# A gated residual in one VectorE pass, one-column statistics on GpSimd, and a new literal order list

## The chip, the cores and the metric

The kernel runs on one core of a Trainium2 chip. The metric is the time of one execution in microseconds on the device (us); lower is better. The engines have short names in the profile: PE is TensorE (matmuls), PEld its weight loads, DVE is VectorE, ACT is ScalarE, POOL is GpSimd, SP is SyncE, which issues nearly all DMA transfers.

## The reference

The input x has 2048 tokens of 640 channels, in fp32. Two layers follow one another, each made of a gated long convolution (A) and a two-matmul MLP (B), each with a layer norm ahead and a residual around it:

```python
def _layernorm(x, axis=-1, eps=1e-5):
    m = jnp.mean(x, axis=axis, keepdims=True)
    v = jnp.var(x, axis=axis, keepdims=True)
    return (x - m) / jnp.sqrt(v + eps)
def _A_ref(q, k, v, shift_k, ssm_k, ssm_D):
    # k_shift: causal depthwise convolution of k, 4 taps
    kv = k_shift * v
    # y: causal depthwise convolution of kv with ssm_k, 2048 taps, by FFT
    y = y + kv * ssm_D[None, None, :]
    return q * y
def _B_ref(x, w1, w2):
    h = jnp.maximum(jnp.einsum("bsd,df->bsf", x, w1), 0)
    return jnp.einsum("bsf,fd->bsd", h, w2)

x = A_q
x = x + _A_ref(_layernorm(x), A_k, A_v, A_shift_k, A_ssm_k, A_ssm_D)
x = x + _B_ref(_layernorm(x), B_w1, B_w2)
x = x + _A_ref(_layernorm(x), A_k, A_v, A_shift_k, A_ssm_k, A_ssm_D)
x = x + _B_ref(_layernorm(x), B_w1, B_w2)
```

The convolution's result y does not depend on x, so both layers use the same y. w1 is 640 x 1728 and w2 is 1728 x 640.

## The kernel before, in words

**Tiles and stages.** The tokens are cut into 8 chunks of 256, each chunk into two halves of 128 tokens (the 128 partitions); channels lie along the free dimension, 640 columns. The statistics of a layer norm are therefore single columns: one number for each token.

- `transform` (tiles kt, acc, tp, sd, pt, sh, pr, at; hf, hr, gs, pg, ob, gt) brings k, v and the long filter into transform space, unit by unit (a chunk and some of its five blocks of 128 channels). `products` multiplies and accumulates there on DVE (pd, pacc; the factors of earlier chunks come back from DRAM as Ax and Gx), and brings y back (u, pq, ys). For chunk 0 ("direct") y is used on the spot; otherwise it is written to DRAM (Y) and read back as the tile y when it is needed; the last blocks of a chunk can be taken straight from ys (`near`).
- `norms` and `wsplit` (ws, w, "ones" sums) scale the MLP weights and split them into fp16 pairs. The MLP runs as three fp16 matmuls per product (high x high, high x low, low x high).
- `prep` makes one gated residual and the input of the following MLP: `stats` of the norm of A, the gate, the residual, `stats` of the norm of B, the split of the normed x into two fp16 halves (xh), and its transposition by DMA (xT).
- `main` is one MLP: h = xT w1 in 14 blocks (1728 = 13 x 128 + 64), each evicted from PSUM by a ReLU on ACT (hh) and a subtraction on DVE (the low half, hl, or for some blocks a combined form, both at line L1494), then o and oc = hh w2, added into x on DVE (L1585). For chunks 6 and 7 a form with fewer block products is used (ha, hs, gs, ek; L1268).

There are 20 mains, n = 0 to 19: chunks 0 and 1 in halves (layer 0 half 0, layer 0 half 1, layer 1 half 0, layer 1 half 1, for each chunk), and then the pairs (2,3), (4,5), (6,7), where each pair does layer 0 for both chunks and then layer 1.

**`stats`.** For each norm ACT makes negm (minus the mean, from row sums), ssq (a pass of squares of 640 columns into the scratch tile jk, with its row sum) and std (square root); DVE takes the reciprocal; then ACT refines 1/sqrt by one Newton step in one- and two-column passes (var, rstd, var, rstd, nmr; L1079 to L1083), one for each half where the scale is a column. ACT ends with the pass xn = r x + nmr (L1093), the normed x. There are tiles of both norms, A and B (xnA, xnB).

**The gate.** DVE multiplies xnA by y (L1136; L906 for the direct chunk), and a second DVE pass adds the product to x and sums the rows into sums2 for the norm of B (L1143). The first norm of a chunk in layer 0 gets its row sums from a pass over x on ACT (jq, L1104); in layer 1 the sums come from the additions of the MLP, whose two parts one ACT step adds (sums, L1593).

**Order.** Every operation is registered with `plan` with its engine, its reads, its writes and a priority. `best`/`order` run a list scheduling over them, whose priorities come from a table (RANKS), and `issue` emits all operations in that order. Each engine has one in-order queue: an operation that waits holds up all behind it. POOL's queue holds set-up work and 40 accumulating DMA issues (L554, L668; 20 each), which wait for their inputs there, and two late additions (L1522). At the start PE runs 38 small matmuls on an identity ("spin", L1602), the first 8 matmuls of pg, and 10 and 8 more spins (L1619) around pt, ahead of pr.

Of the kernel before, what the change touches and what calls it, by code (L numbers as in the profile page):

```python
# [1747 lines left out]
```

## Time and profile before

| what | value |
| --- | --- |
| three runs | 843.01, 843.47, 843.5 us; median 843.47 |
| profiled execution, span on the core | 841.6 us |
| median over that span | 1.9 us |
| instructions in the profile | 20268 |
| granted PE clock | 1.00 in every stage |
| DMA | 181.69 MB, 216 GB/s on average |

The span of the profiled execution runs from the first to the last instruction that the profiler recorded; no time of its own for that execution is given beside it, so the span is set against the median of the runs. Four views are used below: the page with the engines' busy time and the chain of work that ended last; the table of waits (who waited for whom: total, times, longest); windows (busy time of PE, PEld, DVE, ACT, POOL, each with its number of instructions, then the granted clock, the DMA share and GB/s); and groups of instructions by line (busy time, mean ns of one, idle time ahead and what ended it). Times are microseconds from the start of the span.

### The profile page before, as it was taken

What the parts mean: (1) busy time and instruction counts of PE and PEld (TensorE: products, weight loads), DVE (VectorE), ACT (ScalarE), POOL (GpSimd) and SP (SyncE); (2) the same over time, 40 slices, a digit from 0 to 9 for tenths busy, and PEclk for the clock granted to TensorE, in tenths of its full rate; (3) what the DMA queues carried; (4) which work ended last, traced back from release to release, by engine and by line L of the source; (5) the groups of instructions that cost most, each with busy time, mean ns of one, the idle gap of its engine ahead of it and who ended that gap; (6) DMA issues with size and microseconds to landing.
All of it is one profiled execution on the core that took longest, in us unless ns stands there. A gap on an engine that the chain in (4) does not pass through costs nothing.

```text
span 841.6 us, 20268 instructions
## 1 busy us (share of the span) xinstructions
PE 833.6 (99%) x8031; PEld 669.3 (80%) x8031; DVE 786.8 (93%) x1431; ACT 522.8 (62%) x1237; POOL 45.5 (5%) x56
## 2 busy tenths in 40 slices
PE   8999999999999999999999999999999999999998
PEld 7987887888888778777787777777777788888887
DVE  6999999999999999999999999999988799998775
ACT  5798887347776586647438574655524487868432
POOL 0000000000002111011110201010000000000000
PEclk9999999999999999999999999999999999999999
DMA  8995877987999997988998967688987466250400
GB/s 300 395 355 170 259 211 226 309 307 257 266 249 266 327 252 212 239 248 221 235 267 238 244 218 182 159 209 256 255 271 268 110 202 141 79 104 2 58 33 33
DMA packets 138145, 181.69 MB, mean 216 GB/s; under 512 B 53825, under 2 KB 95681, under 8 KB 138050
## 3 DMA queue, kind: packets, MB, share of 16 engines
q1 hardware_dynamic: 129586, 169.81, 67.4%
q0 software_dynamic: 8320, 10.49, 7.9%
q8 instruction: 63, 1.03, 0.5%
q14 instruction: 32, 0.26, 0.1%
q10 hardware_dynamic: 144, 0.10, 0.0%
HBM read 124.59 MB, written 34.08 MB: 189 GB/s over the span
## 4 chain that ended last, share of the span: by engine, by line
PE 79%; DVE 12%; DMA 3%; ACT 3%; issue 2%; SPq 0%; DVEq 0%; ACTq 0%
PE o L1268 10%; PE h L1350 8%; PE h L1351 8%; PE h L1353 8%; PE o L1323 7%; PE o L1322 7%; PE o L1325 6%; PE h L1338 4%; PE h L1383 2%; PE hs L1383 2%; PE h L1340 2%; PE oc L1322 2%; PE oc L1323 2%; PE oc L1325 2%; DVE pd L803 2%
## 5 line engine op out<-in xcount | busy, mean ns | idle before, releaser
L1350 PE MATMUL h<-xT,w 128*128 128x256 f16 (+1 forms) x1000 | 229.4, 249 | 0.9 <-DVE hh L1494 0.9
L1353 PE MATMUL h<-xT,w 128*128 128x256 f16 (+1 forms) x1000 | 229.2, 249 | 0.0
L1351 PE MATMUL h<-xT,w 128*128 128x256 f16 (+1 forms) x1000 | 229.2, 249 | 0.0
L1322 PE MATMUL o<-w,hh 128*128 128x512 f16 x336 | 127.3, 379 | 0.0
L1323 PE MATMUL o<-w,hh 128*128 128x512 f16 x336 | 127.3, 379 | 0.0
L808 DVE TENSOR_TENSOR pacc<-pacc,pd 128x1536 f32<-128x1536 f32 (+1 forms) x75 | 123.2, 1642 | 0.5
L1351 PEld LDWEIGHTS <-w 128*128 128x128 f16 x1100 | 107.6, 98 | 16.0 <-issue 1.8
L1350 PEld LDWEIGHTS <-w 128*128 128x128 f16 x1100 | 107.6, 98 | 14.5
L1353 PEld LDWEIGHTS <-w 128*128 128x128 f16 x1000 | 97.8, 98 | 6.3
L1493 ACT ACTIVATE hh<-h 128x512 f16<-128x512 f32 (+1 forms) x97 | 46.9, 485 | 69.1 <-PE h L1353 29.3
L1322 PEld LDWEIGHTS <-hh 128*128 128x128 f16 x672 | 65.7, 98 | 26.5
L1323 PEld LDWEIGHTS <-hh 128*128 128x128 f16 x672 | 65.8, 98 | 25.9
L803 DVE TENSOR_TENSOR pd<-Ax,Gx 128x768 f32<-128x768 f32 x83 | 78.3, 950 | 4.4 <-DMA Gx<-G 4.1
L1325 PE MATMUL o<-w,hl 128*128 128x512 f16 x208 | 78.8, 379 | 0.0
L1322 PE MATMUL oc<-w,hh 128*128 128x128 f16 x336 | 73.8, 220 | 0.0
L1323 PE MATMUL oc<-w,hh 128*128 128x128 f16 x336 | 73.6, 219 | 0.0
L532 ACT ACTIVATE tp<-kt,shs 128x256 f32<-128x256 f32 (+1 forms) x78 | 44.0, 577 | 26.8 <-DVE acc L606 20.8
L1325 PEld LDWEIGHTS <-hl 128*128 128x128 f16 x416 | 40.7, 98 | 24.5
L1338 PE MATMUL h<-xT,w 128*128 128x256 f16 (+1 forms) x400 | 57.9, 251 | 0.0
L1325 PE MATMUL oc<-w,hl 128*128 128x128 f16 x208 | 45.6, 219 | 0.0
L803 DVE TENSOR_TENSOR pd<-at,Gx 128x768 f32<-128x768 f32 x46 | 43.0, 950 | 0.7 <-DMA Gx<-G 0.5
L1338 PEld LDWEIGHTS <-w 128*128 128x128 f16 x400 | 35.9, 98 | 5.1
(284 smaller groups left out, 2010.3 us busy)
## 6 DMA issues: line engine op xcount, KB each, us to landing
Ax<-A SPq DMA_DIRECT2D x89, 384.0 KB, 4.2
Gx<-G SPq DMA_DIRECT2D x89, 384.0 KB, 4.4
A<-at SPq DMA_DIRECT2D x14, 768.0 KB, 6.3
G<-gt SPq DMA_DIRECT2D x14, 768.0 KB, 5.3
ws<-in_w SPq DMA_DIRECT2D x28, 320.0 KB, 6.8
y<-Y SPq DMA_DIRECT2D x22, 320.0 KB, 3.8
x<-in_q SPq DMA_DIRECT2D x16, 320.0 KB, 4.9
gs<-in_hF SPq DMA_DIRECT2D x20, 256.0 KB, 4.4
```

The costliest lines, as they stand in the source:

```text
L532: ACT.activation(o[:, i : i + m], kview(i, m, j), AF.Copy, scale=shs[:, t, j : j + 1])
L803: ew(f"mac{j % POOLMOD}", 768, lambda e, x=dst[i], av=av, gv=gv: e.tensor_mul(x.t, av(), gv()), [ax, gx], [dst[i]], pr_)
L808: dve(768 * (hi - lo), lambda lo=lo, hi=hi, pd=pd: DVE.tensor_add(acc[:, lo:hi], acc[:, lo:hi], pd[:, lo:hi]), [*sums[lo:hi], *dst[lo:hi]] ...
L1268: PE.matmul(b[:, c : c + w], x, y[:, z : z + w], start=done[i] == 1, stop=end, skip_group_check=fin)
L1322: PE.matmul(z, hh[:, c], wh[:, d], start=(j == JS[0] and i == 0 and (h == 0 or s == S[0])), stop=False)
L1323: PE.matmul(z, hh[:, c], wl[:, d], start=False, stop=end and tail)
L1325: PE.matmul(z, hl[:, c], wh[:, d], start=False, stop=end)
L1338: PE.matmul(p[:, z], wh, xv(t, x), start=b and x == 0, stop=e and x == 1)
L1350: PE.matmul(p[:, z], wh, xv(t, 0), start=b, stop=False)
L1351: PE.matmul(p[:, z], wh, xv(t, 1), start=False, stop=tail and e)
L1353: PE.matmul(p[:, z], wl, xv(t, 0), start=False, stop=e)
L1493: act(2 * R, lambda pv_=pv_, hh=hh: ACT.activation(hh.t, pv_(), AF.Relu), [src], [hh], URGENT)
```

## The change

Four things change.

1. *The gated residual.* With m the mean and r the factor of the norm, x + (x - m) r y equals (x - m)(r y + 1) + m. ACT now makes t = r y + 1 out of y (scale r, bias one), in place of the pass xn; DVE makes x <- (x - m) t in one pass with its row sums; the multiplication by y goes. The m is left out of x, since the norm of B does not see it. It is kept in a small tile (`means`, one column for each half and chunk): layer 0 stores it, layer 1 adds its own mean to it, and 16 ACT passes of 640 columns (one for each half of each chunk, priority LATER) add it to x in layer 1, behind the norm of B.
2. *One-column statistics.* negm, the steps of the Newton refinement, nmr, the means and `sums` move from ACT to POOL, 252 operations in all, as `tensor_scalar` and `tensor_tensor` over one or two columns. ACT keeps squares and square root, DVE the reciprocal.
3. *Column sums of the weights.* The matrix of ones for the three matmuls of `norms` becomes bf16, with the upper half of each fp32 value as the other operand.
4. *The order.* The list scheduling and its table are taken out; the order of all operations is a literal permutation (ORDER).

On DVE 44 instructions fewer are issued; on ACT 305 one- and two-column passes and 32 passes xn fewer, and 44 passes t, 16 passes of the mean and one more table load (`ACT_TABLE_LOAD`; the first operation with another function now comes ahead of the first square root). PE's matmuls are the same, apart from point 3. SP issues the same 512 rows.

```diff
-RANKS = (
-    "D*!A2000311ONp91^@>D2mlEH3IGcL3;+!P4ge1T5C9PX5&#nb6aW<f762Cj7yuan8UPyr8~_~v9snNzAOIl%A^;-*BmgA<CIBY@C;$ThF90zBDF7`1E&wV3GypOHH2^jMIsiTZIRHHXK>$MlQUFu{"
...
+ORDER = (
+    "0{{d71po#B2LK2F2>=QJ3jhoN4FC=R4*(DV5dabZEC4S6DF7`1`~Uy|695zd6#xMMDgZD5E&wtBF#tROHUKvOX#fHMJpgS0ZU8?3"
...
+    def table(self):
+        return [self.ops[k] for k in np.frombuffer(base64.b85decode(ORDER), "<u2")]
     def issue(self):
-        out, end = self.best()
-        for o in out:
+        for o in self.table():
...
+    one = keep(const, [P, 1], "one")
+    POOL.memset(one.t, 1.0)
+    means = keep(const, [P, 2 * NC], "means")
...
         if direct:
-            xs, xns, sp0 = first[c]
+            xs, (r, negm), sp0 = first[c]
             for s in range(2):
-                dve(h, lambda s=s: DVE.tensor_mul(xns[s][:, cs], xns[s][:, cs], dst[s][:, cs]), ...)
-                dve(h, lambda s=s: DVE.scalar_tensor_tensor(xs[s][:, cs], xns[s][:, cs], 1.0, xs[s][:, cs], op0=ALU.mult, op1=ALU.add, accum_out=...), ...)
+                t = T(mlp, "xn", 2, [P, h], f"t{c}{s}{t0}")
+                act(h, lambda s=s, t=t: ACT.activation(t.t, dst[s][:, cs], AF.Identity, scale=r[:, s : s + 1], bias=one.t), ...)
+                dve(h, lambda s=s, t=t: DVE.scalar_tensor_tensor(xs[s][:, cs], xs[s][:, cs], negm[:, s : s + 1], t.t, op0=ALU.add, op1=ALU.mult, accum_out=...), ...)
...
-        ones = keep(const, [P, P], "ones")
+        ones = keep(const, [P, P], "ones", BF16)
...
-    def stats(xs, sums, name, S, pr=0, fine=False):
+    def stats(xs, sums, name, S, pr=0, gated=None):
...
-        act(2, lambda: ACT.activation(negm[:, q_], sums[:, q_], AF.Copy, scale=-1.0 / D), [sums], [negm], pr, 0.1)
+        plan.op("POOL", 0.12, lambda: POOL.tensor_scalar(negm[:, q_], sums[:, q_], -1.0 / D, None, op0=ALU.mult), [sums], [negm], pr)
...
-            (0.2, [ssq, heps], [v], lambda: A(v[:, q_], ssq[:, q_], ident_, scale=-0.5 / D, bias=heps.t)),
-            (0.19 * len(S), [v, sd], [r], lambda: [A(r[:, c], v[:, c], ident_, scale=sd[:, c]) for c in cols]),
...
+            ([ssq], v, lambda: TS(V(v), V(ssq), -0.5 / D, -0.5 * EPS, op0=ALU.mult, op1=ALU.add)),
+            ([v, sd], r, lambda: TT(V(r), V(v), V(sd), op=ALU.mult)),
+            ([r, sd], v, lambda: TT(V(v), V(r), V(sd), op=ALU.mult)),
+            ([v], v, lambda: TS(V(v), V(v), 1.5, None, op0=ALU.add)),
+            ([v, sd], r, lambda: TT(V(r), V(v), V(sd), op=ALU.mult)),
...
+        if gated is not None:
...
+                m = MEAN[a]
+                plan.op("POOL", 0.12, lambda: POOL.tensor_sub(m[:, q_], m[:, q_], negm[:, q_]), [negm, m], [m], FILL)
+            return r, negm
...
-                ew("ay", cut, lambda e, s=s, xn=xns[s]: e.tensor_mul(xn[:, 0:cut], ys[s][:, 0:cut], xn[:, 0:cut]), [ys[s], xns[s]], [xns[s]], URGENT)
+                gate_ = lambda o, i, s=s: ACT.activation(o, i, AF.Identity, scale=r[:, s : s + 1], bias=one.t)
+                act(cut, lambda s=s, t=t, gate_=gate_: gate_(t[:, 0:cut], ys[s][:, 0:cut]), [ys[s], r, one], [t], URGENT, 0.18)
...
-                dve(D, lambda s=s, xn=xns[s]: DVE.scalar_tensor_tensor(xs[s].t, xn.t, 1.0, xs[s].t, op0=ALU.mult, op1=ALU.add, accum_out=sums2[:, s : s + 1]), [xns[s], xs[s]], [xs[s], sums2], URGENT, 0.2)
+                dve(D, lambda s=s, t=t: DVE.scalar_tensor_tensor(xs[s].t, xs[s].t, negm[:, s : s + 1], t.t, op0=ALU.add, op1=ALU.mult, accum_out=sums2[:, s : s + 1]), [t, negm, xs[s]], [xs[s], sums2], URGENT, 0.2)
...
+        for s in S if layer else ():
+            act(D, lambda s=s: ACT.activation(xs[s].t, xs[s].t, AF.Identity, bias=MEAN[a][:, s : s + 1]), [xs[s], MEAN[a]], [xs[s]], LATER, 0.1)
...
-            act(2, lambda: [ACT.activation(sums[:, s : s + 1], sp[:, s, 0:1], AF.Identity, bias=sp[:, s, 1:2]) for s in S], [sp], [sums], URGENT, 0.1 + 0.2 * (len(S) - 1))
+            plan.op("POOL", 0.12, lambda: POOL.tensor_add(sums[:, q_], sp[:, q_, 0], sp[:, q_, 1]), [sp], [sums], URGENT)
```

Three places in the queues show what moves. In the names, `A0_1_0` stands for the norm of A of chunk 0, layer 1, half 0; the last number of a name is a serial number, and the line numbers of after are its own.

The first place is that norm on ACT, from its row sums to the pass of 640 columns that DVE needs. Before:

```order
L1593 ACTIVATE sums0_0_0_1467<-sp0_0_0_1448 128x1
L1068 ACTIVATE negmA0_1_0_1469<-sums0_0_0_1467 128x1
L1071 ACTIVATE jkA0_1_00_1476,ssqA0_1_0_1477<-x0_0_222,negmA0_1_0_1469 128x640
L1072 ACTIVATE stdA0_1_0_1487<-ssqA0_1_0_1477,epst_88 128x1
L663 ACTIVATE ob1_2_1489<-pg11_2_1474 128x512
L532 ACTIVATE tp11_4_1502<-kt1_4_1446,shs_94 128x256
L1498 ACTIVATE tl_86<-hb1_1491 64x128
L532 ACTIVATE acc1_4_1517<-kt1_4_1446,shs_94 128x256
L1079 ACTIVATE varA0_1_0_1535<-ssqA0_1_0_1477,heps_90 128x1
L1080 ACTIVATE rstdA0_1_0_1536<-varA0_1_0_1535,stdA0_1_0_1487 128x1
L1081 ACTIVATE varA0_1_0_1535<-rstdA0_1_0_1536,c15_91,stdA0_1_0_1487 128x1
L1082 ACTIVATE rstdA0_1_0_1536<-varA0_1_0_1535,stdA0_1_0_1487 128x1
```

Now, on ACT:

```order
L998 ACTIVATE jkA0_1_00_1451,ssqA0_1_0_1452<-x0_0_219,negmA0_1_0_1417 128x640
L999 ACTIVATE stdA0_1_0_1454<-ssqA0_1_0_1452,epst_88 128x1
L455 ACTIVATE tp11_4_1468<-kt1_4_1389,shs_93 128x256
L616 ACTIVATE sh1_2_1494<-pt1_2_1471 128x512
L373 ACTIVATE cGh_1500<-cG_167 128x512
L1075 ACTIVATE t0_1_00_1512<-y0_1_00_1114,one_90,rstdA0_1_0_1465 128x640
```

and on POOL, whose queue had held no work here:

```order
L1532 TENSOR_TENSOR sums0_0_0_1415<-sp0_0_0_1412 128x1
L995 TENSOR_SCALAR negmA0_1_0_1417<-sums0_0_0_1415 128x1
L1006 TENSOR_SCALAR varA0_1_0_1457<-ssqA0_1_0_1452 128x1
L1007 TENSOR_TENSOR rstdA0_1_0_1465<-varA0_1_0_1457,stdA0_1_0_1454 128x1
L1008 TENSOR_TENSOR varA0_1_0_1457<-rstdA0_1_0_1465,stdA0_1_0_1454 128x1
L1009 TENSOR_SCALAR varA0_1_0_1457<-varA0_1_0_1457 128x1
L1010 TENSOR_TENSOR rstdA0_1_0_1465<-varA0_1_0_1457,stdA0_1_0_1454 128x1
L995 TENSOR_SCALAR negmB0_1_0_1522<-sums20_1_0_1520 128x1
```

The steps from sums to rstd have moved to POOL, and between square root and t ACT's queue has three other passes where it had four and five small steps.

The second place is the gated residual of the same half on DVE, behind the reciprocal. Before:

```order
L1074 RECIPROCAL stdA0_1_0_1487<-stdA0_1_0_1487 128x1
L664 TENSOR_TENSOR gt1_2_1515<-pg01_2_1465,ob1_2_1489 128x2x2x128
L558 TENSOR_TENSOR gs01_4_1543<-hf1_4_1373,hr1_4_1368 128x256
L665 TENSOR_TENSOR gt1_2_1515<-pg01_2_1465,ob1_2_1489 128x2x2x128
L606 TENSOR_TENSOR acc1_4_1517<-acc1_4_1517,tp11_4_1502 128x256
L558 TENSOR_TENSOR gs11_4_1555<-hf1_4_1373,hr1_4_1368 128x256
L675 TENSOR_TENSOR gt1_2_1515<-gt1_2_1515 128x2x256
L1136 TENSOR_TENSOR xnA0_1_00_1553<-y0_1_00_1173,xnA0_1_00_1553 128x640
L606 TENSOR_TENSOR acc1_4_1517<-acc1_4_1517,tp21_4_1580 128x256
L1143 SCALAR_TENSOR_TENSOR x0_0_222,sums20_1_0_1600<-xnA0_1_00_1553,x0_0_222 128x640
```

Now:

```order
L1001 RECIPROCAL stdA0_1_0_1454<-stdA0_1_0_1454 128x1
L481 TENSOR_TENSOR gs01_4_1492<-hf1_4_1380,hr1_4_1442 128x256
L1433 SCALAR_TENSOR_TENSOR hh1_3_1445<-h1_3_1391,hh1_3_1445 128x256
L481 TENSOR_TENSOR gs11_4_1502<-hf1_4_1380,hr1_4_1442 128x256
L726 TENSOR_TENSOR pd1_0_2_1448<-at1_0_1214,Gx1_0_0_1_1153 128x768
L1080 SCALAR_TENSOR_TENSOR x0_0_219,sums20_1_0_1520<-x0_0_219,negmA0_1_0_1417,t0_1_00_1512 128x640
```

The two passes have become one, with four other passes between the reciprocal and it where there were seven.

The third place is the start of PE. Behind 38 spins it had:

```order
L636 MATMUL pg00_0_213<-hf0_0_163,cG_151 128x2x128 x4
L636 MATMUL pg10_0_228<-hf0_0_163,cG_151 128x2x128
L636 MATMUL pg10_0_228<-hf0_0_163,cX_200 128x2x128
...
L683 MATMUL pt0_0_260<-ident_76,sd0_0_243 128x128 x4
...
L698 MATMUL pr00_0_285<-sh0_0_279,cM_204 128x2x128 x2
```

and behind 19 spins it now has:

```order
L559 MATMUL pg00_0_185<-hf0_0_165,cG_167 128x2x128 x4
L559 MATMUL pg10_0_198<-hf0_0_165,cG_167 128x2x128
L559 MATMUL pg10_0_198<-hf0_0_165,cX_177 128x2x128
...
L606 MATMUL pt0_0_226<-ident_76,sd0_0_215 128x128 x4
...
L559 MATMUL pg10_2_249<-hf0_2_217,cG_167 128x2x128
...
L621 MATMUL pr00_0_310<-sh0_0_242,cM_221 128x2x128 x2
```

Half of the spins ahead of pg have moved behind it: five stand between pg and pt, four behind pt, and 28 between the next two matmuls of pg and pr. The list of loads on SP changes there too: the first piece of k and the filter now stand ahead of cG, x of the first half one place earlier, cM three places later.

More of the change, by code (lines that the diff above doesn't have):

```diff
@@ L364, in issue @@
             o.fn()
-        return end
 @with_exitstack
@@ L1633, in early @@
         sums = load_x(a)
-        first[a] = (X[a], stats(X[a], sums, f"A{a}_0", both, URGENT, True), [keep(const, [P, 1, 3], f"sp{a}_{s}") for s in range(2)])
+        first[a] = (X[a], stats(X[a], sums, f"A{a}_0", both, URGENT, (a, 0)), [keep(const, [P, 1, 3], f"sp{a}_{s}") for s in range(2)])
     early(0)
```

316 lines of the change are left out of this document (122 added, 194 removed).

## The prediction

> **What bounds the kernel now.** I read the page first, for the engines' shares and the chain that ended last; then what TensorE (PE) waits for; then busy time by stage; then the chain where it leaves PE. First the page's lines on engines and on the chain:
>
> ```profile
> PE 833.6 (99%) x8031; PEld 669.3 (80%) x8031; DVE 786.8 (93%) x1431; ACT 522.8 (62%) x1237; POOL 45.5 (5%) x56
> PE 79%; DVE 12%; DMA 3%; ACT 3%; issue 2%; SPq 0%; DVEq 0%; ACTq 0%
> ```
>
> PE is busy for 833.6 of 841.6 us, so at most 8.0 us of visible idle time is there to be won, whatever VectorE (DVE) is spared, as long as the matmuls stay. They do: the change alters no matmul but three small ones. Next, all that PE waits for:
>
> ```profile
> PE spin L1602 <- POOL heps L435: 1.9, 1, 1.9
> PE h L1350 <- DVE hh L1494: 0.9, 2, 0.6
> PE pg L636 <- DVE hf L538: 0.8, 2, 0.4
> PE oc L1325 <- DVE hh L1494: 0.3, 1, 0.3
> PE pr L698 <- ACT sh L693: 0.2, 1, 0.2
> ```
>
> The 1.9 is the start before anything can run, 0.8 + 0.2 belong to the start-up of the convolution, and 0.9 + 0.3 = 1.2 us are waits for DVE in the steady part. The stages (columns after the comma: PE, PEld, DVE, ACT, POOL) show where:
>
> ```profile
> 0.00:20.00 20.00, 17.04 (x116) 14.97 (x117) 13.08 (x31) 11.25 (x25) 1.81 (x14) 1.00 0.87 296
> 80.00:100.00 20.00, 19.70 (x183) 15.59 (x182) 19.46 (x41) 16.56 (x40) 0.00 (x0) 1.00 0.75 239
> 120.00:140.00 20.00, 19.12 (x236) 16.51 (x234) 18.78 (x39) 14.37 (x39) 0.00 (x0) 1.00 0.69 209
> 200.00:400.00 200.00, 199.94 (x1893) 157.26 (x1893) 198.14 (x313) 136.50 (x327) 19.94 (x20) 1.00 0.93 256
> 400.00:680.00 280.00, 280.00 (x2323) 213.47 (x2321) 264.12 (x378) 146.92 (x345) 22.03 (x21) 1.00 0.83 226
> 760.00:842.00 82.00, 77.75 (x950) 67.65 (x947) 59.54 (x167) 38.02 (x91) 1.69 (x2) 1.00 0.16 32
> ```
>
> DVE is nearly full from 80 to 400 us, but from 200 us on PE is full too. PE's holes lie in the first 20 us (2.96), in 80–140 (0.30 + 0.88 = 1.18) and in the last window (4.25, mostly the stores after the last matmul). The chain that ended last runs through ACT and DVE from 80 to about 235 us and through PE from there; its pieces at the first hole (start, length, what), and the removed multiplies that it holds later:
>
> ```profile
> 79.95 0.21 ACT negmA L1068
> 80.18 0.93 ACT jkA L1071 x2
> 83.14 0.19 ACT varA L1079
> 83.36 0.30 ACT rstdA L1080
> ...
> 84.43 0.30 ACT nmrA L1083
> 84.76 0.93 ACT xnA L1093
> 85.72 0.82 DVE xnA L1136
> 86.94 0.60 issue
> 108.68 0.74 DVE xnA L1136
> 132.81 1.28 DVE xnA L1136 x2
> 199.87 0.74 DVE xnA L1136
> ```
>
> The hole itself, at the end of that 1.28 (start, length, engine, what; in brackets the idle time before):
>
> ```profile
> 131.14 1.75 DVE L808 TENSOR_TENSOR pacc<-pacc,pd 128x1536 f32<-128x1536 f32 x1
> ...
> 134.01 0.41 DVE L1494 SCALAR_TENSOR_TENSOR hh<-h,hh 128x256 f16<-128x256 f32 x1
> 134.48 0.22 PE L1350 MATMUL h<-xT,w 128*128 128x128 f16 x1 [0.62 <-DVE hh L1494]
> 134.48 0.10 PEld L1351 LDWEIGHTS <-w 128*128 128x128 f16 x1 [0.90 <-issue]
> ```
>
> The split of h (L1494), for which PE waits, stands on DVE right behind two of the multiplies that go. The weight loads idle 0.90 where PE's column says 0.62: idle time counts only from the modelled end of the last matmul, so the real hole is up to 0.28 larger, and holes shorter than that do not show.
>
> **The change, part by part.** *DVE.* Prices of the pass that goes and of the one that stays:
>
> ```profile
> L1136 DVE TENSOR_TENSOR xnA<-y,xnA 128x640 f32<-128x640 f32 x22 | 17.7, 819 | 0.9 <-ACT xnA L1093 0.8
> L1143 DVE SCALAR_TENSOR_TENSOR x<-xnA,x 128x640 f32<-128x640 f32 x30 | 24.4, 815 | 0.0
> ```
>
> 22 full multiplies are 17.7 us; 22 narrower ones (128 to 512 columns) I count by columns: 4 of 384, 4 of 512, 8 of 256, 6 of 128 is 6,400 columns, or 10 times 640, so 10 x 0.82 = 8.2 us. Some 26 us of DVE work goes in all. The pass x <- x + xnA becomes (x - mean) x t, in the same form and size, at 815 ns: no change. Off the path 26 us are worth nothing; on it they are worth PE's holes. Both visible waits (1.2) are for DVE, and the chain holds 0.82 + 0.74 + 1.28 + 0.74 = 3.58 us of removed passes before 235 us. So the term has the ends 0 (another DVE instruction ends last there) and -3.6. With three recorded waits, each up to 0.28 short, the holes are 1.2 + 3 x 0.28 = 2.0, and small ones come on top; I take **-2.4**. Late next there is PE itself.
>
> *ACT.* 305 one- and two-column steps leave. In the chain above they take from 83.14 to 84.73, 1.6 us for one half of a chunk. The normalising pass (0.93) is replaced by t = r y + 1 of the same width: equal. Sixteen passes x + mean (640 columns, so about 0.93 each, 15 us) come late in layer 1 at a low priority. ACT is 62% busy and 136.50 of 200 in the fullest long stage; the steps that left cover them. Without that cover, one such pass ahead of the ReLU eviction would delay PE by 0.93 us. A second table load, at the start, lies in ACT's idle time before 20 us. I count 0.
>
> *GpSimd (POOL).* 252 small operations come, in one queue with 40 DMA issues. The trace has no such operation; its nearest rows:
>
> ```profile
> L1522 POOL TENSOR_TENSOR x<-x,ek 128x320 f32<-128x320 f32 x2 | 1.7, 862 | 213.6 <-ACT ek L1519 213.6
> L433 POOL MEMSET epst<- 128x1 f32 x1 | 0.1, 98 | 0.0
> L554 POOL DMA_DIRECT2D gs<-hr x20 | 20.0, 1001 | 328.4 <-DVE x L1585 214.4 <-ACT hr L553 44.1 <-DVE gt L664 34.2
> 835.57 1.13 DVE L1431 SCALAR_TENSOR_TENSOR x<-o,winv,x 128x320 f32<-128x320 f32 x2
> ```
>
> One column costs between 0.10 (a write of one column) and 0.86 (two inputs, 320 columns). A linear reading of the two, 0.10 + 2/320 of the rest, stays near 0.1; a two-input step has some start-up, so I take 0.15. Five steps are then 0.75 us against ACT's 1.6, about 0.8 us less on each stretch from squares to t. At 0.86 they would be 4.3, or 2.7 us more. Behind an accumulating DMA of L554 a step waits 1.0 us for its issue at most, if that DMA's inputs have landed; the stages show no POOL work between 80 and 140 us, where PE's holes are, and 20 instructions in 200 to 400, where it has none. A DMA standing ahead with late inputs would hold the steps longer. Both I count 0.
>
> The Trainium skill speaks against this part: "SBUF — State Buffer", section "Who interferes with whom", says that a DVE instruction with two SBUF inputs contends with a GpSimd instruction that reads SBUF, whoever issues first keeping the shared port to its end. By this rule DVE, which is nearly full with such passes, would hold up most small steps by half a pass or so, which is rival B below. In this trace the two L1431 passes that run at 835.57, over the start of the two-input L1522, take 1.13 together, their usual 0.54 each; but one of their inputs is an output of PE, so no run here shows the case.
>
> *Order and start.* The literal order puts 19 of the 38 warm-up matmuls ahead of the first convolution matmuls, the others behind. Rows of the start:
>
> ```profile
> 1.95 4.24 PE L1602 MATMUL spin<-ident 128*128 128x128 f16 x38 [1.95 <-POOL heps L435]
> 6.12 0.41 DVE L538 TENSOR_TENSOR hf<-hf,dDs 1x256 f32<-1x256 f32 x1
> 6.58 2.43 PE L636 MATMUL pg<-hf,cG 128*128 128x256 f32 x10 [0.39 <-DVE hf L538]
> 10.14 0.72 PE L1619 MATMUL spin<-ident 128*128 128x128 f16 x10
> ```
>
> The first spins come 4.24/38 = 0.11 us apart, the ten at 10.14 about 0.06: PE starts at half speed. Its queue's 16 records of pg run from 6.58 to 10.14, 3.56 us. With 19 spins it is quiet from about 4.1 to 6.6; were it to run all of pg cold, that adds up to 3.56. About 1.0 of it is made good by fewer idle spins ahead of the first use (18 stood between 10 and 13 us) and by the 1.0 us of waits there. Bounds 0 to +2.5; I take +0.5, since DVE, not PE, carries 20 to 40 us. The loads of x for the first half stand one place earlier and cM later, which the same bound covers. The three bf16 column sums save at most three fp32 passes of 0.1: -0.2. At the end the last DVE pass has 128 columns either way: 0.
>
> The Trainium skill, "TensorE: Matmul & The Clock Gate", section "What's actually happening", gives about 3.4 us of sustained activity before full speed; the trace agrees so far that the spins of the first 4.2 us are at half. By that rule 19 spins (about 2.1 us) do not suffice, and pg would begin cold.
>
> The sum: 841.6 - 2.4 + 0.5 - 0.2 = 839.5 in the profiled execution. The median of the runs is 843.47, 1.9 above its span, so **841.4**; since each stretch from squares to t also shortens by 0.8, which the holes not seen in the columns may return, I round down to **841.0**.
>
> **The rivals.** *A: no change.* The holes at 94 and 134 us are where h and o need DVE; with another order a different pass ends last there (a 1.75-us accumulation stood ahead of the multiplies at 131.14), and a cold start of +2.5 eats what is left. Against it: 26 us of work leave DVE in front of these holes. Time: 841.6 + 2.5 - 2.4 + 1.9 = 843.6.
>
> *B: slower, by the small steps.* One main stage passes 14 POOL operations on its path (the sums, a negm and five steps for the gated norm; a negm, five steps and nmr for the other), in place of 1.6 + 1.6 us of ACT steps and three of 0.21 (negm, negm, sums), together some 3.8, and of a multiply of 0.82. It decides at (3.8 + 0.82)/14 = 0.33 us per step. At 0.6 each, the stretch is 14 x 0.27 = 3.8 us longer. In 80–140 us, where the next half waits for it, two such stretches would show, and the saved 2.4 goes; with half of it covered by other work, 843.5 + 3.8 = 847.3. For it speaks that nothing in the trace reads one column on POOL; against it the 98-ns row.
>
> *C: a larger gain.* All 3.58 us of the chain's passes come back, start-up stays equal: 841.6 - 3.6 - 0.4 + 1.9 = 839.5.
>
> *D: slower by the start.* A cold PE and the moved loads cost the full +3.5 and the holes stay: 847.
>
> **How the numbers follow.** The forecast with C, 838.5 to 841.7: 0.55. A: 0.21. B: 0.15. D: 0.09. A measurement of this kernel can tell 0.2%, 1.7 us: below 841.8 is faster, above 845.2 slower. Faster takes the 0.55 and a little of A (0.03): 0.58; same is A and the small ends of B and D: 0.21; slower 0.21. The range 838.5 to 846.5 leaves out the upper half of B and D, and gains over 5 us, together 2 in 10. The likeliest one's own range is 839 to 841.8.
>
> **What would show it.** Right: no wait of h or oc for DVE hh over 0.3 us in 80–140; DVE busy near 760 us; ACT without one-column steps; POOL small operations below 0.3 us each; PE's chain starting before 200 us. Cold start: the first pg records twice as far apart as 3.56/16 = 0.22. Wrong: ACT passes t waiting for POOL rstd by more than 2 us from the reciprocal; h waiting for DVE with a new pass ahead; more than 4 us of PE idle in the first 20.

## The result, and the profile after

The changed kernel takes 915.96 us (median of 5 runs, 915.06 to 920.63) against 843.47 us before (5 runs, 843.01 to 843.84): a ratio of 1.0873, 95% interval 1.0853 to 1.0894. It is 72 us slower, where 2.5 us less were forecast and the range ended at 846.5. Its profiled execution has a span of 913.3 us.

The page's lines on engines and on the chain that ended last:

```profile
PE 855.1 (94%) x8028; PEld 670.8 (73%) x8028; DVE 778.8 (85%) x1387; ACT 466.6 (51%) x932; POOL 167.0 (18%) x310
DVE 19%; PE 9%; DMA 6%; ACT 4%; issue 4%; POOL 2%; SPq 0%; DVEq 0%; POOLq 0%; ACTq 0%
```

No engine is full any more: DVE has fallen from 93% to 85%, ACT from 62% to 51%, and PE from 99% to 94%. PE stands still for 58.2 us where it stood for 8.0, and its busy time, for nearly the same matmuls, is 21.5 us longer (855.1 against 833.6); together that is the 71.7 us of span. The chain, which had been PE for 79% of the span, is now followed through only part of it (its shares add up to 44%) and passes DVE more than PE: this kernel waits. What PE waits for (the five longest of a list that had five entries in all before):

```profile
PE oc L1264 <- DVE hl L1433: 9.7, 6, 3.4
PE h L1277 <- DMA xT<-xh: 8.9, 6, 3.7
PE h L1289 <- DVE hh L1433: 5.1, 5, 2.4
PE hb L1289 <- DVE hh L1433: 4.0, 2, 3.0
PE pg L582 <- DVE ys L805: 2.6, 2, 1.7
```

And what ACT waits for, the four long entries with POOL:

```profile
ACT jkA L998 <- POOL negmA L995: 31.1, 15, 8.4
ACT t L1075 <- POOL rstdA L1010: 26.9, 15, 4.6
ACT xnB L1031 <- POOL nmrB L1013: 26.4, 11, 4.6
ACT jkB L998 <- POOL negmB L995: 19.6, 11, 4.5
```

ACT stands for 31.1 + 26.9 + 26.4 + 19.6 = 104 us in front of a POOL step, with the ReLU evictions that PE and DVE need queued behind. By stage (PE, PEld, DVE, ACT, POOL, then the granted clock):

```profile
0.00:20.00 20.00, 16.64 (x105) 14.36 (x106) 12.37 (x28) 9.94 (x18) 2.00 (x14) 1.00 0.83 260
80.00:100.00 20.00, 17.72 (x184) 14.03 (x182) 17.29 (x34) 11.84 (x27) 8.16 (x15) 1.00 0.57 196
120.00:140.00 20.00, 17.68 (x194) 13.99 (x192) 16.11 (x33) 17.07 (x41) 5.40 (x12) 1.00 0.78 218
200.00:400.00 200.00, 183.14 (x1751) 141.79 (x1750) 173.73 (x271) 101.27 (x203) 55.47 (x89) 0.97 0.83 231
400.00:680.00 280.00, 263.49 (x2133) 197.75 (x2132) 250.28 (x351) 128.00 (x246) 64.72 (x97) 0.99 0.80 216
```

PE now has holes in every stage: 16.9 us in 200 to 400, where it had 0.06, and 16.5 in 400 to 680, where it had none. The norm of chunk 0, layer 1, half 0 (the chain from 79.95 to 86 us of before) shows what a step does; start, length, engine, what:

```profile
82.49 0.95 DVE L726 TENSOR_TENSOR pd<-at,Gx 128x768 f32<-128x768 f32 x1
82.54 0.96 POOL L1006 TENSOR_SCALAR varA<-ssqA 128x1 f32<-128x1 f32 x1 [1.04 <-ACT jkA L998]
...
84.63 0.41 DVE L1433 SCALAR_TENSOR_TENSOR hh<-h,hh 128x256 f16<-128x256 f32 x1
84.83 0.19 POOL L1008 TENSOR_TENSOR varA<-rstdA,stdA 128x1 f32<-128x1 f32 x1
...
85.29 0.95 DVE L726 TENSOR_TENSOR pd<-at,Gx 128x768 f32<-128x768 f32 x1
85.54 0.75 POOL L1010 TENSOR_TENSOR rstdA<-varA,stdA 128x1 f32<-128x1 f32 x1
86.32 0.92 ACT L1075 ACTIVATE t<-y,one,rstdA 128x640 f32<-128x640 f32 x1 [1.95 <-POOL rstdA L1010]
```

A step that starts while DVE multiplies two tiles from SBUF (82.54, 85.54) ends 0.05 us behind that pass (82.49 + 0.95 = 83.44 against 83.50; 86.24 against 86.29). One that starts beside hh, which reads h from PSUM (84.83), takes 0.19. Over all 255 small steps of the trace: about 50 start with no DVE pass in flight, median 0.195 us; about 48 beside a pass that reads PSUM, median 0.196; about 157 beside a pass with both inputs in SBUF, mean 0.66, and their median end is 0.05 behind that pass. (The description of the change counts 252 of them. It also says that 305 one- and two-column passes leave ACT: that is the fall of all of ACT's instructions, and 334 such passes left.)

### The profile page after: what moved, and what is told of

It reads as the page before. It is cut to its first block, busy times and chain, and to the rows that moved or that the text cites. A ratio compares the mean times of both kernels' runs of the same rounds, so it can differ in the third digit from the quotient of the medians.

```text
span 913.3 us, 20165 instructions
## 1 busy us (share of the span) xinstructions
PE 855.1 (94%) x8028; PEld 670.8 (73%) x8028; DVE 778.8 (85%) x1387; ACT 466.6 (51%) x932; POOL 167.0 (18%) x310
## 5 line engine op out<-in xcount | busy, mean ns | idle before, releaser
L1532 POOL TENSOR_TENSOR sums<-sp 128x2 f32<-128x2 f32 (+1 forms) x10 | 6.3, 631 | 243.3 <-DVE x L1524 190.5
```

## The experiments

Theory 1: the small steps on POOL wait for DVE's passes, and ACT, DVE and PE wait behind them. Theory 2: the literal order is slow by itself. Theory 3: the pass t and the new residual pass are what is late.

**Steps on ACT, in the literal order.**

```diff
-            plan.op("POOL", 0.12, f, rd, [wr], pr)
+            plan.op("ACT", 0.12, f, rd, [wr], pr)   # steps as ACT.activation, one column each
```

> The changed kernel with all its one- and two-column steps (negm, the refinement, nmr, means, sums) given back to ACT at the same places of the same literal order; the single pass of the gated residual, the pass t and the order stay. Theory 1 (small POOL steps wait for DVE passes with two inputs in SBUF, and ACT, DVE and PE wait behind them): nearly all of the 72 us goes, 840 to 850 us. Theory 2 (the literal order is slow by itself): still over 880 us. Theory 3 (t out of y on ACT and the new residual pass are what is late): still over 880 us.

Measured: 913.74 us, ratio 1.0821 (1.0803 to 1.0839): as slow as on POOL.

**Steps on DVE, in the literal order.**

```diff
-        TS, TT = POOL.tensor_scalar, POOL.tensor_tensor
+        TS, TT = DVE.tensor_scalar, DVE.tensor_tensor
...
+            plan.op("DVE", 0.12, f, rd, [wr], pr)
```

> The changed kernel with the same steps as DVE instructions at the same places of the order. 252 steps on the fullest engine at some 0.07 to 0.1 us each are 18 to 25 us of DVE work, about what the removed multiplies gave. Theory 1: 838 to 850 us, near the run with ACT. Theory 2 and theory 3: over 880 us.

Measured: 948.63 us, ratio 1.1243 (1.1225 to 1.1261), slower still. A step takes some 0.16 us there, not the 0.07 to 0.1 expected, and DVE's busy time rises from 778.8 to 808.4 us; how much of the loss is that price, this run doesn't separate. ACT's waits in these two runs, of the steps on ACT first:

```profile
ACT sums L1535 <- DVE x L1527: 27.8, 9, 5.7
ACT negmB L998 <- DVE x L1083: 25.8, 15, 4.6
```

and of the steps on DVE:

```profile
ACT xnB L1031 <- DVE nmrB L1013: 47.5, 15, 10.1
ACT t L1075 <- DVE rstdA L1010: 45.0, 17, 10.0
```

On POOL a step at the head of its queue held up only other steps; on ACT `sums` and `negm` now hold up all of ACT while they wait for DVE, and on DVE each step of a chain stands behind whole passes. So these two runs don't price the order by itself: they put the steps where the order had no place for them. Both runs missed what theory 1 expected and met what theories 2 and 3 expected (over 880 us), but for this reason they don't yet decide between them.

**Steps on POOL, in the order of before.** The order that the list scheduling of before gives was written down literally; the steps are at the places that ACT had them.

```diff
-        act(2, lambda: ACT.activation(negm[:, q_], sums[:, q_], AF.Copy, scale=-1.0 / D), [sums], [negm], pr, 0.1)
+        plan.op("POOL", 0.12, lambda: POOL.tensor_scalar(negm[:, q_], sums[:, q_], -1.0 / D, None, op0=ALU.mult), [sums], [negm], pr)
...
-            act(0, lambda: [f() for *_, f in steps], ...)
+            plan.op("POOL", 0.7, lambda: [f() for *_, f in steps], ...)   # steps as POOL.tensor_scalar, tensor_tensor
```

> The kernel before, its own order written down literally, with nothing changed but that negm, the refinement, nmr and sums are POOL instructions at the places where ACT had them. Theory 1: 880 to 930 us, steps of 0.4 us or more in the mean, ending right behind the DVE pass in flight. Theory 2 or 3: 840 to 850 us.

Measured: 891.68 us, ratio 1.0555 (1.0533 to 1.0577). The steps on POOL alone cost 48 us, with nothing else changed; the 255 steps take 149.9 us in all, 0.59 in the mean. ACT waits here for POOL's nmrB and nmrA above all:

```profile
ACT xnB L1014 <- POOL nmrB L1004: 53.5, 16, 6.3
ACT xnA L1014 <- POOL nmrA L1004: 44.8, 16, 7.2
```

**The one pass alone, in the order of before.** Statistics stay on ACT; t stands where the multiply stood. The passes of the mean and the bf16 column sums come along; the order list is the same as in the run before this one.

```diff
-                dve(h, lambda s=s: DVE.tensor_mul(xns[s][:, cs], xns[s][:, cs], dst[s][:, cs]), ...)
+                act(h, lambda s=s: ACT.activation(xns[s][:, cs], dst[s][:, cs], AF.Identity, scale=r[:, s : s + 1], bias=one.t), ...)
```

> The kernel before, its own order written down literally, with the gated residual alone changed: t on ACT at the place of the multiply, one DVE pass, means kept and added in layer 1 right behind the high half of xh; statistics stay on ACT; the ones of the column sums are bf16 as in the changed kernel. 26 us of DVE work go. Theory 1: 838 to 845 us (the prediction's term for DVE was -2.4). Theory 3: over 860 us. A tie with before would say that DVE's spared time is not where PE's holes end.

Measured: 843.85 us (11 runs), ratio 1.0008 (0.9999 to 1.0017): no difference. Theory 3 falls, and writing the order of before down literally costs nothing that can be told. DVE is less busy (767.7 us, 91%), and part of PE's holes has closed:

```profile
80.00:100.00 20.00, 20.00 (x191) 15.97 (x190) 19.30 (x40) 17.22 (x43) 0.00 (x0) 1.00 0.78 248
120.00:140.00 20.00, 19.72 (x242) 16.92 (x241) 18.25 (x37) 15.67 (x44) 0.00 (x0) 1.00 0.66 217
```

PE's longest waits of that run, the start aside:

```profile
PE pg L555 <- DVE hf L457: 1.0, 2, 0.7
PE h L1319 <- DVE ha L1330: 0.9, 1, 0.9
```

0.30 + 0.60 = 0.9 us came back in these two stages; a new wait of 0.9 (h for ha, a form that only chunks 6 and 7 have) took as much.

**A small step by itself.**

> No part of the reference: six stretches of 24 instructions, each stretch fenced from the next, that price one dependent one-column step on POOL (c = c x d) alone, beside DVE passes of 768 columns with two inputs in SBUF, beside DVE passes of 512 columns with one input in PSUM, beside ACT passes of 768 columns, and one-column steps on DVE itself between its passes. Theory 1 (shared port): 0.2 us alone, beside PSUM input and beside ACT; some 0.5 to 0.95 us each beside two SBUF inputs, each ending just behind a DVE pass. Rival (a POOL step is slow in itself or by its semaphores): the same 0.4 us or more in all stretches.

The body of the kernel is six such loops, the second and third of them:

```python
for _ in range(24): DVE.tensor_tensor(o1, a, b, op=ALU.mult)                      # 768 columns, SBUF and SBUF
for _ in range(24): POOL.tensor_tensor(c[:, 0:1], c[:, 0:1], d[:, 0:1], op=ALU.mult)
...
for _ in range(24): DVE.tensor_tensor(o1[:, 0:512], pz, b[:, 0:512], op=ALU.mult)  # PSUM and SBUF
for _ in range(24): POOL.tensor_tensor(c[:, 0:1], c[:, 0:1], d[:, 0:1], op=ALU.mult)
```

One execution; the stretches in order of time (start, length of the 24 together):

```profile
5.89 6.35 POOL L387 TENSOR_TENSOR c<-c,d 128x1 f32<-128x1 f32 x24
...
13.01 23.80 DVE L402 TENSOR_TENSOR o<-a,b 128x768 f32<-128x768 f32 x24 [0.30 <-POOL c L392]
13.05 23.81 POOL L387 TENSOR_TENSOR c<-c,d 128x1 f32<-128x1 f32 x24
...
37.64 17.37 DVE L408 TENSOR_TENSOR o<-pz,b 128x512 f32<-128x512 f32 x24 [0.30 <-POOL c L392]
37.68 6.35 POOL L387 TENSOR_TENSOR c<-c,d 128x1 f32<-128x1 f32 x24
...
55.83 23.80 DVE L414 TENSOR_TENSOR o<-a,b 128x768 f32<-128x768 f32 x24 [0.30 <-POOL c L392]
...
81.07 20.95 ACT L419 ACTIVATE f<-e 128x768 f32<-128x768 f32 x24
...
81.45 6.36 POOL L387 TENSOR_TENSOR c<-c,d 128x1 f32<-128x1 f32 x24
```

A chain of steps goes at 6.35/24 = 0.26 us a step alone, beside PSUM input, and beside ACT; beside passes with two SBUF inputs it goes at 23.81/24 = 0.99, exactly one step for each DVE pass. DVE loses nothing: 23.80 with the steps and without. By the Trainium skill, "SBUF — State Buffer", section "Who interferes with whom", a DVE instruction with two SBUF inputs contends with a GpSimd instruction that reads SBUF, because its second input comes through the read interface that the two share. The measurement agrees with the rule: 0.99 us a step there, 0.26 beside one SBUF input. The loop with one-column steps on DVE told nothing on that form, since the two kinds did not alternate there.

**The literal order with the steps left out.**

```diff
-        plan.op("POOL", 0.12, lambda: POOL.tensor_scalar(negm[:, q_], ...), [sums], [negm], pr)
+        gone()   # an operation that issues nothing; likewise for the other steps
...
-            act(D, lambda s=s, jk=jk: ACT.activation(jk.t, xs[s].t, AF.Square, bias=negm[:, s : s + 1], ...), ...)
+            act(D, lambda s=s, jk=jk: ACT.activation(jk.t, xs[s].t, AF.Square, bias=sc(s), ...), ...)   # sc(s) is a column of zeros
```

> The changed kernel with its literal order, and the 252 small steps left out: means and the refinement of the root are not computed, squares and t take a column of zeros for the mean and the plain reciprocal for the factor; all 640-column passes and all matmuls stay in their order. No small step can wait for anything. Theory 1 alone (the steps on POOL are all of the loss): 838 to 846 us. Theory 2 (the order's queues wait by themselves): 870 us or more. If both, in between.

Measured: 868.33 us (863.02 to 872.81), ratio 1.0286 (1.0242 to 1.0331). With no small step at all the order is still 24 us behind before. So there are two causes.

**The one pass with the order planned anew by before's table.** The edit is shown against the run of the one pass alone.

```diff
-        for o in self.table():
+        for o in self.best()[0]:   # list scheduling with RANKS, on the costs of the new passes
```

> The kernel before with the gated residual in one DVE pass and its statistics on ACT as in the run before, but with its own list scheduling run anew, with the same table of priorities and the costs of the new passes, instead of its order written down. If DVE's 26 us can be turned into time at all: 838 to 842 us. If PE's work is the bound whatever DVE does: 842 to 845 us. If the table is tuned to one set of costs: slower, 846 to 860 us.

Measured: 846.96 us, ratio 1.0040 (1.0026 to 1.0054): slower than with the old order kept (843.85). The spared DVE time isn't turned into time in this way either.

**The changed kernel, steps on ACT, in a plain replanned order.**

```diff
-        for o in self.table():
+        for o in self.order()[0]:   # list scheduling, each operation's own class as its priority
```

> The changed kernel with its small steps on ACT, in the order that the list scheduling of the kernel before gives for them with plain priorities (each operation's class, then its place in the program), in place of the literal order. Theory 2 (the literal order is what keeps this at 914 us): 845 to 880 us. If the one pass with t on ACT is itself the cause: over 900 us again.

Measured: 850.06 us, ratio 1.0074 (1.0059 to 1.0089). With the same operations on the same engines as in the first run, the order alone is worth 914 - 850 = 64 us.

**The replanned order with steps left out, and with steps on POOL.** The edit is the table ORDER alone, in the run without steps and in the changed kernel.

> The same work as the run of the changed kernel without its small steps (means and refinement left out), in the order of the replanned kernel (850 us with steps on ACT) in place of the literal order. If the literal order costs some 24 us by itself: 838 to 848 us, against 868. If that run was slow for another reason (the pass t, the mean passes, the new residual): 860 us or more here too.

Measured: 848.55 us, ratio 1.0063 (1.0046 to 1.0080).

> All of the changed kernel, small steps on POOL too, in that same replanned order in place of the literal one. If the two causes add up (steps on POOL some 47 us, as in the kernel before, order some 20 to 24): 885 to 905 us. If the steps on POOL cost little once the order is right: under 865 us. If the order makes nothing of it: 910 us or more.

Measured: 877.21 us, ratio 1.0398 (1.0374 to 1.0422), below the 885 that adding up gave. The two causes together, medians in us:

| order | no steps | steps on ACT | steps on POOL | on DVE |
| --- | --- | --- | --- | --- |
| of before, one pass | | 843.85 | | |
| of before, two passes | | 843.47 | 891.68 | |
| replanned | 848.55 | 850.06 | 877.21 | |
| literal | 868.33 | 913.74 | 915.96 | 948.63 |

Steps on POOL cost 29 us in the replanned order and 48 in the literal one and in that of before. The literal order costs 20 us without steps and 39 with them on POOL. They don't add: steps on POOL cost more in the literal order than in the replanned one. That a late step costs more where the order leaves less room behind it fits this, but no run varied the room alone.

How much room, I read from the traces as the time between the end of the split of xh on DVE and the first matmul h that needs it, for the two layers of chunks 2 to 5: 12.1 to 25.2 us in the replanned order without steps, 4.8 to 15.2 in the literal one (likewise), 2.3 to 13.2 in the order of before. Before has as little room and loses nothing, so little room by itself is not what costs the 20 us; that it makes a late step dear fits the 48 us there and the 29 in the replanned order. What waits in the literal order without steps, and the page's chain of that run:

```profile
PE h L1263 <- DMA xT<-xh: 4.8, 7, 1.6
DVE pd L729 <- DMA Gx<-G: 17.4, 11, 5.1
```

```profile
PE 51%; DVE 29%; DMA 10%; issue 4%; ACT 4%; SPq 1%; DVEq 0%; ACTq 0%
```

The same two of the replanned order without steps:

```profile
DVE pd L725 <- DMA Gx<-G: 8.8, 7, 4.2
```

```profile
PE 79%; DVE 13%; issue 3%; DMA 3%; ACT 2%; POOL 0%; DVEq 0%; POOLq 0%; ACTq 0%; SPq 0%
```

Loads of Gx come late for DVE, and transposes of xh late for PE. Before had 4.6 us of waits for Gx, and neither it nor the replanned order any wait for transposes of xh. In these two profiled executions the orders are 14.3 us apart (spans 861.2 and 846.9), not 20. In the literal order without steps the chain runs through loads between 625 and 655 us:

```profile
625.67 5.20 DMA Gx<-G
...
633.50 4.97 DMA Gx<-G
...
644.38 4.92 DMA out_dram<-x
...
649.36 5.02 DMA x<-in_q
```

There the load of x waits until the store of the previous x has landed, at the head of SP's queue, with loads of Gx behind it. That these late transfers are what the order costs is read from the waits, not shown by a run: which operations would have to move was not tried.

**Where along the program the order costs.** The table ORDER again, cut after 1350 operations.

> The work without small steps again; the first 1350 of 3947 operations (to about 234 us, where the norm of chunk 2 begins) in the replanned order, the others in the literal order. If the literal order loses at the start and in the halves (theory: cold PE, tight first norms): about 850 us. If it loses in the pairs, through late loads and late norms all along: about 860 to 866 us.

Measured: 863.53 us (860.62 to 867.45): 15.0 above the replanned order.

> The complement: the first 1350 operations in the literal order, the others in the replanned one. If the loss is at the start and in the halves: 860 to 868 us; if in the pairs: 850 to 856 us. The two losses together should be the 20 us between 848.6 and 868.3, unless the seam itself costs.

Measured: 855.09 us (853.46 to 857.39): 6.5 above it. 15.0 + 6.5 = 21.5 against 868.33 - 848.55 = 19.8, so the parts add up within their spread. By the medians the pairs carry about 15 of the 20.

> The literal order without small steps, with 38 warm-up matmuls ahead of the first pg instead of 19 and nothing else moved. If the cold PE at the start costs to the end: the first records of pg 0.22 us apart, not 0.43, and 1 to 2.5 us less than 868.3. If DVE carries the start: no difference over 0.5 us.

Measured: 866.15 us (863.14 to 866.97) against 868.33 (863.02 to 872.81): within the spread, nothing shown. The first 16 records of pg are warm here (0.22 apart), but the first h comes at 46.3 us, not before the 45.4 of the run without this edit; PE then waits for DVE (from the table of waits), and its clock falls to 0.58 between 12 and 16 us (from the windows, the third number from the end):

```profile
PE pt L605 <- DVE sd L534: 1.9, 1, 1.9
```

```profile
12.00:16.00 4.00, 3.72 (x23) 2.94 (x22) 3.93 (x10) 2.48 (x6) 0.00 (x0) 0.58 0.98 314
```

No version ran faster than before.

## Why the prediction was wrong

**The step that failed first: the price of a small step on POOL.** I took 0.15 us, "about 0.8 us less on each stretch". Alone a step takes 0.19 us and a chain 0.26 a step; the 255 steps of the changed kernel mean 0.49 (124.4 us in all), and 0.66 in the mean beside DVE passes with two SBUF inputs, which about 157 of them met. A sign named for being wrong is there: the pass t waits for POOL's rstd 15 times, 26.9 us in all and up to 4.6. Rival B named this mechanism, its deciding point (0.33 us) and 0.6 as its price, and got 15 in 100. The clue was in the text: DVE is nearly full, and nearly all its costly passes read two tiles from SBUF, so a step alone is the rare case. I weighed the 98-ns write of one column as evidence against, though it reads nothing.

**The second: how often the longer stretch shows.** Rival B let two stretches show, half covered, for +3.8 us. 157 steps that are 0.66 - 0.20 = 0.46 us longer make 72 us of longer steps (that the kernel lost 72 us too is a coincidence); 48 us came out at the end in the literal order. In the other two orders the steps took 149.9 us (that of before) and 143.8 (replanned) where 255 x 0.195 is 49.7, so they were longer by 100 and 94 us, of which 48 and 29 came out. From 200 us on I had counted on cover, since PE had no hole there. A full PE doesn't say that what feeds it has room: the xh split ended 2.3 to 13.2 us ahead of its first matmul in that stretch. And a step that waits holds ACT's whole queue (104 us of waits at its head), not its own chain alone.

**The third: the order counted as nothing but its start.** Rival D, the start at +3.5, was the only price of the literal order, with A's "a different pass ends last there". Without any small step that order costs 20 us more than a plain replanning, about 15 of them in the pairs; its trace shows waits for loads and transposes that I had not priced: I compared how much work stood ahead of each matmul on each engine, and not when a load could be issued.

**DVE's spared time: -2.4 predicted, nothing measured.** The reading that DVE ended the holes at 80 to 140 us was right (0.9 of 1.18 us came back there with the one pass alone), and the bound of at most 8 us on any gain too. The step "late next there is PE itself" was not: other waits of that size came. Rival C falls. Its price also missed that the new pass is dearer:

```profile
L1080 DVE SCALAR_TENSOR_TENSOR x<-x,negmA,t 128x640 f32<-128x640 f32 x30 | 25.9, 881 | 11.4 <-ACT t L1075 11.3
```

881 ns against 815 ("no change"), 30 x 0.066 = 2.0 us. In the run of the one pass alone, with no steps on POOL, it is 879, so POOL isn't why. The profile of before had the price in another pass of this form, with a column as its scalar:

```profile
L977 DVE SCALAR_TENSOR_TENSOR w<-ws,wsc,w 128x640 f16<-128x640 f32 x28 | 23.9, 878 | 0.3 <-ACT w L976 0.3
```

**The cold start: right in kind.** In the changed kernel the first records of pg stand 0.43 us apart for eleven intervals, until 10.8 us:

```profile
5.57 4.63 PE L559 MATMUL pg<-hf,cG 128*128 128x256 f32 x10 [1.41 <-DVE hf L461]
10.00 1.00 PE L559 MATMUL pg<-hf,cX 128*128 128x256 f32 x2
```

The rule of the Trainium skill, "TensorE: Matmul & The Clock Gate", section "What's actually happening", that the prediction quotes agrees in kind: 19 spins of 2.2 us were not enough. Its 3.4 us is not one fixed length here: full pace came 5.2 us after the first pg in this run and 3.3 in the one without steps, and in before all 38 spins, 4.2 us, stayed at half, which the prediction took as agreeing. The windows print a clock of 1.00 for these 20 us all the same; the half pace shows in the spacing alone. Warm, it changed no time that could be told; "DVE, not PE, carries 20 to 40 us" held. The first h came at 45.3 us instead of 41.5, also at 45.4 without steps and at 46.3 with the warm start, but at 41.8 with the one pass in the order of before: that is the order.

**Not settled.** The bf16 column sums were not timed by themselves. Why the replanned order without steps is 5 us behind before, and which moves in the literal order make the loads late, stays open; as does the split of the 72 us in the changed kernel, since the two causes share 19 us. Of PE's 21.5 us of longer busy time, the first 16 records of pg (6.1 us instead of 3.6) and the lower clock told below are some 10; the rest was not traced.

## What to carry to other kernels

Price a small operation on GpSimd by what VectorE does meanwhile, not by its own length: beside passes with two SBUF inputs a chain advances one step for each such pass. Before moving steps of a chain off an engine, measure how early its result is there today; a full last engine hides nothing if its input comes 2 to 13 us ahead. A fixed order belongs to the timing and the engines it was made for: change either, and compare with a plain replanning before judging the change itself.

## What the runs showed of the hardware

In the small loops DVE's passes did not wait for POOL's steps: 24 of them take 23.80 us either way. `scalar_tensor_tensor` with a column of SBUF as its scalar took 0.88 us on 640 columns where the one with a constant took 0.82.

The clock that PE is granted can fall in the middle of the program, not at its start alone: 0.97 in 200 to 400 us of the changed kernel, 1.00 there before. In windows of 20 us it is 0.91 in four (240 to 260, 280 to 300, 340 to 360, 520 to 540), where PE stands still for 2.5 to 3.9 us, and 1.00 in all others up to 900, also in 220 to 240, where PE stands still for 3.95; so idle time goes with it, but these sums don't tell when it falls. An estimate from the four windows, 4 x 0.09 x 20 us, is 7 us of clock, part of which falls on idle time. It also goes with the spread of one program: without steps in the literal order, the execution of 863.02 us had a mean clock of 1.000, that of 872.81 one of 0.994.
